# A chunked delta-rule kernel: the last step of the triangular inverse replaced by one residual correction

## The chip, the cores and the metric

The kernel runs on one core of one Trainium2 chip. A core has TensorE (PE, the matrix unit), VectorE (DVE), ScalarE (ACT), GpSimd (POOL) and SyncE (SP), each with its own instruction queue worked off in order, and 16 DMA engines. The metric is the device time of one execution in microseconds. Before the change it is 259.1 us (median of the runs; the lowest is 258.44 us).

## The reference: what is computed

For each of 4 × 8 heads with 768 time steps and 48 dimensions a state matrix is updated by the delta rule, and the outputs of all heads go through a feed-forward block of 384 → 2048 → 384 with a tanh-approximated GELU.

```python
k_n = k / (np.linalg.norm(k, axis=-1, keepdims=True) + 1e-06)
for t in range(S):
    y[:, :, t] = np.einsum('bhd,bhde->bhe', q[:, :, t], state)
    v_old = np.einsum('bhde,bhd->bhe', state, kt)
    state = state + bt[:, :, :, None] * np.einsum('bhd,bhe->bhde', kt, vt - v_old)
...
h = x @ w_in
g = 0.5 * h * (1.0 + np.tanh(c * (h + 0.044715 * h * h * h)))
return (g @ w_out).astype(np.float32)
```

`kt` is the normalised key of step t, `vt` the value, `bt` the scalar beta. Inputs and output are float32.

## The kernel before, in words

**Tiling.** Time is cut into 12 chunks of 64 steps (C = 64). A chunk holds 32 heads; 16 of them form a *unit*, two heads side by side on the two halves of the 128 partitions, so that there are 24 units, u = 2c and 2c + 1 for chunk c. Names in the code end in the unit (`A3.13`) or the chunk (`U.6`).

**Preparation of a unit (`load`, `norms`, `prep`).** q, k and v are loaded by DMA, the norms of k are computed, k is scaled, and everything is transposed, by PE (`T`, `kT`) or by a DMA transpose (`turn`). PE then makes the Gram matrices of the chunk: `G2` (keys with keys, its lower triangle kept by a DVE mask copy into `ln`, line 528) and `G` (keys with keys and with queries, upper triangle, mask copy into `wp`; in the first units separately, with `GQ` and `wpq`, or the ACT copy `wqa` and the POOL product `wqb`).

**The inverse.** Inside a chunk the delta rule is a triangular system (I + L) U = R. Its inverse is found by Newton's iteration in 5 steps, for every unit. The iterate is kept as a block-diagonal matrix `bd` (128 x 128 for each of 8 head pairs). `X10` and `X11` write the start (line 558, POOL, or line 560, DVE). Each step i is: `A{i}`, eight PE products of `bd` with a Gram matrix (line 569); `rt{i}`, a DVE instruction that forms 2I minus that (line 581); `B{i}`, eight products of `bd` with it (line 569); and copies out of PSUM back into `bd`: `bde` (two half copies, ACT or DVE, line 326), `bdf` (line 332), or `xi` (one copy) and then two `bdc` on POOL or DVE (line 611). Steps 4 and 5 work only on the columns that aren't exact yet: step 4 on 48 of 64, step 5 on 32. A form `J`, `C`, `rj` replaces `A`, `rt` in some places: PE puts 2I into PSUM first (line 587), and ACT or DVE copies.

**The chunk chain (`chain`).** From the state S of the chunk before: `K` (line 641) multiplies the state with the keys, `R` (DVE, line 654) forms the right-hand side `rb`, `U` (16 PE products of `bd` with `rb`, line 664) solves the system, `Un` copies it into `ub`, `S` (line 676) and `Sn` (DVE, line 683) form the next state, `Q` and `O` (lines 641 and 689) the output, `On` copies it, and it is transposed by PE (`X`, line 701, copy `xT`) or by DMA (`turnx`, line 706).

**The feed-forward block (`mlp`).** For each chunk 16 `up` products (line 718, three matmuls each), 4 `gelu` on ACT (line 722), 8 `down` (line 729, four matmuls each), copies `Z` and the DMAs out. The weights W1 and W2 are loaded by POOL's DMA queue (`w1`, `w2`, lines 435 and 437).

**The order.** The class `Flow` collects all operations with what they read and write. The string `ORDER` at the top (lines 17 to 105) lists all of them in one sequence; a suffix names the engine that is chosen (`:a` ACT, `:d` DVE, `:g` POOL, `:s` SP) or the PSUM bank (`@5`). Each engine's queue is that sequence cut down to its own operations, and `Flow.emit` adds the semaphore waits. There is no reordering at run time: an operation that waits holds up all behind it on its engine. PSUM has 8 banks; an operation that takes a bank waits until the last reader of the bank's earlier content is done. The `fill` products at the start only keep PE busy.

## Time and profile before

| | before |
|---|---|
| median of the runs | 259.1 us |
| profiled execution | 259.73 us |
| its span, first to last instruction | 258.0 us |
| granted TensorE clock, mean | 0.992 |
| busy: PE / DVE / ACT / POOL | 241.1 / 206.2 / 191.1 / 140.8 us |
| instructions | 12268 |

The profile shows one execution. The busy time of an engine is the union of its instructions; a PE matmul is drawn with its whole passage through the array, so that neighbours overlap, and the cost of a group on PE is read from the distance between starts. Idle time is put down to the instruction whose semaphore ended it ("<-"), and "issue" is a wait for which the profile shows no releaser. Line numbers are those of the kernel before. "PEld" is the loading of weights into the array, "SPq" and "ACTq" the queues that issue DMAs.

### The profile page before, as it was taken

What the parts mean: (1) busy time and instruction counts of PE and PEld (TensorE: products, weight loads), DVE (VectorE), ACT (ScalarE), POOL (GpSimd) and SP (SyncE); (2) the same over time, 40 slices, a digit from 0 to 9 for tenths busy, and PEclk for the clock granted to TensorE, in tenths of its full rate; (3) what the DMA queues carried; (4) which work ended last, traced back from release to release, by engine and by line L of the source; (5) the groups of instructions that cost most, each with busy time, mean ns of one, the idle gap of its engine ahead of it and who ended that gap; (6) DMA issues with size and microseconds to landing.
All of it is one profiled execution on the core that took longest, in us unless ns stands there. A gap on an engine that the chain in (4) does not pass through costs nothing.

```text
span 258.0 us, 12268 instructions
## 1 busy us (share of the span) xinstructions
PE 241.1 (93%) x5490; PEld 189.0 (73%) x5497; DVE 206.2 (80%) x354; ACT 191.1 (74%) x305; POOL 140.8 (55%) x205
## 2 busy tenths in 40 slices
PE   7878689979999999999999999999999999999994
PEld 2455568758877987887877887778868878878672
DVE  7889899979978989999889868889888889875100
ACT  4777789699987886996887887777946957655352
POOL 6679883889636797674595678455441322400000
PEclk9999979999999999999999999999999999999999
DMA  4999999994795997969939792239377123002122
GB/s 81 192 189 194 217 202 198 198 169 79 142 138 107 188 141 137 187 131 157 200 72 140 165 177 58 51 64 149 85 104 150 33 51 107 3 5 64 33 60 62
DMA packets 116788, 31.46 MB, mean 122 GB/s; under 512 B 110848, under 2 KB 115968, under 8 KB 116736
## 3 DMA queue, kind: packets, MB, share of 16 engines
q1 hardware_dynamic: 81136, 19.03, 47.6%
q10 hardware_dynamic: 32720, 8.51, 17.8%
q0 software_dynamic: 2880, 3.15, 7.2%
q8 instruction: 43, 0.70, 1.1%
q14 instruction: 9, 0.07, 0.1%
HBM read 20.64 MB, written 4.72 MB: 98 GB/s over the span
## 4 chain that ended last, share of the span: by engine, by line
PE 78%; DMA 6%; POOL 4%; ACT 4%; SPq 2%; DVE 2%; issue 2%; ACTq 1%; POOLq 0%
PE ps L729 24%; PE ps L718 23%; PE ps L569 20%; DMA kraw<-in_k_dram 3%; PE ps L524 3%; PE ps L641 3%; DMA qraw<-in_q_dram 2%; SPq L426 2%; PE ps L664 2%; PE ps L689 1%; PE ps L676 1%; ACT bd L326 1%; DVE rt L581 1%; POOL bd L558 1%; ACTq L426 1%
## 5 line engine op out<-in xcount | busy, mean ns | idle before, releaser
L326 ACT ACTIVATE bd<-ps 64x512 bf16<-64x512 f32 x122 | 70.6, 589 | 27.9 <-PE ps L569 26.0
L718 PE MATMUL ps<-xT,W 128*128 128x256 bf16 x576 | 77.5, 273 | 0.4 <-issue 0.2
L729 PE MATMUL ps<-W,gT 128*128 128x384 bf16 x384 | 74.1, 326 | 1.0 <-ACT wp L326 1.0
L722 ACT ACTIVATE gT<-ps 128x1024 bf16<-128x1024 f32 x48 | 48.0, 1019 | 14.9 <-PE ps L718 14.2
L581 DVE TENSOR_TENSOR rt<-ps,two 128x512 bf16<-128x512 f32 x70 | 47.5, 685 | 10.5 <-PE ps L569 9.4
L718 PEld LDWEIGHTS ps<-xT,W 128*128 128x128 bf16 x576 | 50.1, 98 | 6.9 <-issue 0.4
L729 PEld LDWEIGHTS ps<-W,gT 128*128 128x128 bf16 x384 | 32.8, 98 | 17.7 <-ACT wp L326 1.2
L558 POOL TENSOR_SCALAR_AFFINE_SELECT bd<-ln 64x512 bf16<-64x512 bf16 x40 | 26.6, 669 | 21.5 <-DVE ln L528 18.8
L611 POOL COPY bd<-xi 64x256 f32<-64x256 f32 x36 | 14.8, 415 | 34.7 <-ACT xi L326 26.9
L452 POOL TENSOR_TENSOR nrm<-nrm,half 128x16 f32<-128x16 f32 x9 | 26.3, 2920 | 6.5 <-DVE nrm L450 6.4
L569 PE MATMUL ps<-rt,bd 128*128 128x64 bf16 x576 | 28.1, 194 | 1.7 <-DVE rt L581 1.0
L569 PE MATMUL ps<-wp,bd 128*128 128x64 bf16 (+1 forms) x576 | 27.0, 188 | 1.9 <-ACT bd L332 0.6
L569 PEld LDWEIGHTS ps<-rt,bd 128*128 128x128 bf16 x576 | 23.3, 98 | 6.3 <-DVE rt L581 2.3
L528 DVE CAST_PREDICATED wp<-mup,ps 128x1024 bf16<-128x1024 uint16 (+1 forms) x25 | 27.6, 1107 | 0.5 <-PE ps L524 0.4
L569 PEld LDWEIGHTS ps<-wp,bd 128*128 128x128 bf16 x576 | 23.0, 97 | 5.0 <-ACT bd L326 0.7
L326 DVE CAST bd<-ps 64x512 bf16<-64x512 f32 x35 | 23.9, 685 | 2.6 <-PE ps L569 2.1
L581 DVE TENSOR_TENSOR rl<-ps,two 128x384 bf16<-128x384 f32 (+1 forms) x48 | 23.0, 486 | 3.6 <-PE ps L569 2.9
L479 POOL TENSOR_TENSOR tok<-kraw,nrm 128x384 bf16<-128x384 f32 x21 | 17.6, 840 | 8.9 <-PE ps L676 8.4
L332 ACT ACTIVATE bd<-ps,up 128x512 bf16<-128x512 f32 x29 | 19.6, 675 | 0.9 <-issue 0.4
L569 PE MATMUL ps<-ln,bd 128*128 128x64 bf16 (+1 forms) x384 | 18.7, 190 | 0.9 <-ACT bd L326 0.6
L528 DVE CAST_PREDICATED ln<-mlo,ps 128x512 bf16<-128x512 uint16 x24 | 16.4, 682 | 3.6 <-PE ps L524 3.3
L569 PE MATMUL ps<-rl,bd 128*128 128x64 bf16 x384 | 19.0, 194 | 0.2
(104 smaller groups left out, 344.1 us busy)
## 6 DMA issues: line engine op xcount, KB each, us to landing
qraw<-in_q_dram SPq DMA_DIRECT2D x16, 192.0 KB, 5.1
kraw<-in_k_dram SPq DMA_DIRECT2D x27, 96.0 KB, 4.0
vraw<-in_v_dram SPq DMA_DIRECT2D x26, 96.0 KB, 4.6
out_dram<-ob ACTq DMA_DIRECT2D x13, 192.0 KB, 3.2
vraw<-in_v_dram ACTq DMA_DIRECT2D x22, 96.0 KB, 4.2
out_dram<-ob SPq DMA_DIRECT2D x9, 192.0 KB, 3.6
kraw<-in_k_dram ACTq DMA_DIRECT2D x17, 96.0 KB, 4.3
qraw<-in_q_dram ACTq DMA_DIRECT2D x8, 192.0 KB, 5.9
```

What stands on the lines that cost most here:

```text
L326: return e.activation(out, in_, ACT.Copy) if e is nc.scalar else e.tensor_copy(out, in_)
L332: return e.activation(out, in_, ACT.Copy, scale=up1[:, 0:1]) if e is nc.scalar else e.tensor_scalar(out, in_, up1[:, 0:1], None, op0=ALU.mult)
L452: if e is nc.scalar else e.tensor_tensor(nr[:, 1, hx], nr[:, 0, hx], half[:, hx], ALU.pow), reads=[nrn, "half"] + ["one", "roots"] * (c < ...
L479: A(("dve", "pool"), op("kb"), lambda e, P: e.tensor_tensor(kb, kr, nr[:, 5, hx].unsqueeze(2).to_broadcast(full), ALU.mult), reads=[f"kraw ...
L528: return e.copy_predicated(out.rearrange("p (x g) t -> p x g t", x=2), mask[:, 0:wd].bitcast(U16).unsqueeze(1).unsqueeze(1).to_broadcast([ ...
L558: A(("pool", "dve"), op(f"X1{a}"), lambda e, P, src=ln[m][hf(a), :, :], dst=bd[b_][hf(a), :, hf(a)], a=a: e.affine_select(out=dst, in_=src ...
L569: ins = e.matmul(P(name)[:, C * h + cs.start:C * h + cs.stop], bd[b_][:, h, :], rhs[:, h, cs], **kw)
L581: A(("dve",), op(f"rt{i}"), lambda e, P, i=i, cs=cs, cn=cn, r_=r_: e.tensor_tensor(r_[:, :, cs], P(ps(f"A{i}")).rearrange("p (h t) -> p h ...
L611: A(("pool", "dve"), op(f"bdc{i}{a}"), lambda e, P, src=xi[i_][hf(a), :, :], dst=bd[b_][hf(a), :, hf(a)]: e.tensor_copy(dst.bitcast(F32), ...
L718: ins = e.matmul(P(ph)[:, 256 * f:256 * f + 256].rearrange("p (x t) -> p x t", x=2), W1[:, j, 128 * (i + f):128 * (i + f) + 128], x_[:, :, ...
L722: A(("act",), f"gelu{i // 4}.{c}", lambda e, P, i=i, ph=ph: e.activation(g_[:, i:i + 4, :], P(ph).rearrange("p (f t) -> p f t", f=4), ACT. ...
L729: ins = e.matmul(P(po)[:, 0:DM], g_[:, f, 128 * b:128 * b + 128], W2[:, f, :], start=(f == 0), stop=(f == FC - 1))
```

## The change

`RES` names the chunks 1 to 11. For their units the iteration makes 4 steps instead of 5. The start of the iteration comes from the upper mask copy (`wp`) instead of the lower one (`ln`), so that the sides alternate the other way round and step 4 works on the upper 48 columns. In the chain `U` now gives a first solution, which `Ua` (ACT or DVE) copies to `ub`. `M` (function `left`, 32 PE products of 64 x 64 weights) multiplies it with the masked Gram matrix in `wp`, `rd` (DVE) adds that to the right-hand side `rb`, so that `rb` becomes the residual, and `V` (the 16 products of `U` again) adds its correction into the PSUM banks of `U`, which stay taken until `Un` has copied them. Chunk 0 keeps its five steps.

`ORDER` is replaced as a whole: 1661 operations instead of 1727, in another sequence, with other choices of engine and bank. Among the choices: 5 `J` forms instead of 2, 7 `X` instead of 5 (so 5 `turnx` instead of 7), `wpq` on DVE for all of the first four units instead of `wqa` and `wqb` for three of them, 31 `fill` instead of 37, and many loads issued by SP that ACT issued before. The diff shows a few lines of the order and then the code.

```diff
--- before
+++ after
...
-up1.7 bdc50.17:d bdc51.17:g A2.19@5 up2.7 U.8@0 gelu2.7 bdc21.18:d Un.8:a A3.18@4 rt2.19 up4.7@6 up3.7 B2.19@5 rt3.18 S.8@0 B3.18@4 gelu0.7 up5.7 bde21.19:d
-On.8:a ln.21 qb.22:a G2.20@2 rt3.19 G.21@0 down02.7 ln.20 wp.21 B3.19@4 wp.20 down10.7@2 down11.7 X10.21:g A4.18@1 down12.7 bdf30.19:a rt4.18 X11.21:g A1.21@6
...
+rt3.14 k11.00:a gelu0.5 up8.5@4 rt2.15 up9.5 Ua.6:a M.6@6 v9.10:s up10.5 ln.16 k11.11:s out00.3:s B2.15@0 B3.14@1 up11.5 rd.6 xi3.14:d V.6 sq.10:g bdc30.14:g
...
+xi2.18:d up11.7 gelu2.7 bdc20.18:d up1.7 out00.5:s bdc21.18:d up2.7 up3.7 A2.19@0 pow.11 qb.22:g A3.18@1 U.8@6 up4.7@2 gelu0.7 rt2.19 B2.19@0 up5.7 rt3.18
+Ua.8:a vs.9:g B3.18@1 M.8@4 xi2.19:d bdc20.19:d xi3.18:a up6.7 rd.8 up7.7 Q.8@0 eps.11:g gelu1.7 qb.21:g V.8 Un.8:a bdc21.19:g bdc30.18:d A3.19@5 down10.7@4
...
+bdc40.23:d U.11@2 up1.10 Ua.11:a up2.10 up3.10 Z1.9:d Z0.9:a M.11@4 out11.9:s up4.10@6 up5.10 up6.10 rd.11 up7.10 gelu0.10 up8.10@0 V.11 up9.10 gelu1.10
...
@@ -270,6 +265,7 @@
     SPLIT = 4
     APART = 2
     ROOTS = 3
+    RES = range(1, NC)
     NR, NP, NB, NN, NI, NX, NG = 3, 6, 6, 4, 3, 3, 3
 
     F = Flow()
@@ -306,8 +302,8 @@
         tmpl = sb("tmpl", [128, 2 * C])
         bd = sb("bd", [128, H, 128], BF16, NB)
         rt = sb("rt", [128, H, C], BF16, NN)
-        rls = [sb(f"rl{i}_", [128, NN * H, C]) for i in range(2)]
-        rl = [[t[:, H * i:H * i + H, :] for i in range(NN)] for t in rls]
+        rls = [sb(f"rl{i}_", [128, (2 if i else NN + 2) * H, C]) for i in range(2)]
+        rl = [[t[:, H * i:H * i + H, :] for i in range(t.shape[1] // H)] for t in rls]
         xi = sb("xi", [128, H, C], BF16, NI)
         rs = sb("rs", [128, 2, 2, 4, D], BF16, 2)
         us = sb("us", [128, 2, 2, 4, D], BF16, 2)
@@ -374,11 +370,12 @@
                       e is not nc.gpsimd else e.tensor_copy(t[s][:, :, :].bitcast(F32), tmpl[:, 0:w].bitcast(F32).unsqueeze(1).to_broadcast([128, H, w // 2])),
                       reads=["tmpl", "tmplz"], writes=[f"{y}{s}" for y in n])
             for i in range(0 if s else 2):
-                lo, kc_ = 16 + 16 * i, slice(0, 32) if i else slice(C - 16, C)
-                A(EV, f"ladj{lo}", lambda e, P, i=i, lo=lo, kc_=kc_: e.activation(
-                    rls[i][:, :, kc_], tmpl[:, kc_].unsqueeze(1).to_broadcast([128, NN * H, lo]), ACT.Copy, scale=-1.0) if e is nc.scalar else
-                  e.tensor_scalar(rls[i][:, :, kc_], tmpl[:, kc_].unsqueeze(1).to_broadcast([128, NN * H, lo]), -1.0, None, op0=ALU.mult),
-                  reads=["tmpl"], writes=[f"rl{lo}{y}" for y in range(NN)])
+                lo = 16 + 16 * i
+                for y0, y1, kc_ in ((0, 2, slice(0, 32)),) if i else ((NN, NN + 2, slice(C - 16, C)), (0, NN, slice(0, 16))):
+                    A(EV, f"ladj{lo}{y0}", lambda e, P, i=i, lo=lo, kc_=kc_, y0=y0, y1=y1: e.activation(
+                        rls[i][:, H * y0:H * y1, kc_], tmpl[:, kc_].unsqueeze(1).to_broadcast([128, (y1 - y0) * H, lo]), ACT.Copy, scale=-1.0) if e is nc.scalar else
+                      e.tensor_scalar(rls[i][:, H * y0:H * y1, kc_], tmpl[:, kc_].unsqueeze(1).to_broadcast([128, (y1 - y0) * H, lo]), -1.0, None, op0=ALU.mult),
+                      reads=["tmpl"], writes=[f"rl{lo}{y}" for y in range(y0, y1)])
             if s < NB:
                 A(("dve", "pool"), f"bdz{s}", lambda e, P: e.memset(bd[s][:, :, :].bitcast(F32), 0.0), writes=[f"bd0{s}", f"bd1{s}"])
 
@@ -548,19 +545,19 @@
 
             bds = [f"bd{a}{b_}" for a in range(2)]
             xis = f"xi{i_}"
-            for i in range(1, 6):
+            for i in range(1, 5 if c in RES else 6):
                 if tiled:
                     if i == 1:
                         A(("dve", "pool"), op("X1"), lambda e, P: e.tensor_tensor(
                             xi[i_][:, :, :], ln[m][:, :, :], twob[:, :].unsqueeze(1).to_broadcast([128, H, C]), ALU.add), reads=[w("ln"), "twob"], writes=[xis])
                 elif i == 1:
                     for a in range(2):
-                        A(("pool", "dve"), op(f"X1{a}"), lambda e, P, src=ln[m][hf(a), :, :], dst=bd[b_][hf(a), :, hf(a)], a=a: e.affine_select(
+                        A(("pool", "dve"), op(f"X1{a}"), lambda e, P, src=(wp[s][hf(a), :, 0:C] if c in RES else ln[m][hf(a), :, :]), dst=bd[b_][hf(a), :, hf(a)], a=a: e.affine_select(
                             out=dst, in_=src, compare_op=ALU.not_equal, fill=1.0, base=0, pattern=[[0, H], [-1, C]],
                             channel_multiplier=1) if e is nc.gpsimd else e.tensor_tensor(
                             dst, src, twob[hf(a), :].unsqueeze(1).to_broadcast([64, H, C]), ALU.add),
-                          reads=[w("ln"), "twob"], writes=[bds[a]], upper=a == 1)
-                con, conn = (wp[s][:, :, 0:C], n("wpm")) if i % 2 else (ln[m], w("ln"))
+                          reads=[n("wpm") if c in RES else w("ln"), "twob"], writes=[bds[a]], upper=a == 1)
+                con, conn = (wp[s][:, :, 0:C], n("wpm")) if (i + (c in RES)) % 2 else (ln[m], w("ln"))
 
                 def product(e, P, name, rhs, cs, more=False):
                     kw = dict(start=False, stop=True, skip_group_check=True) if more else {}
@@ -572,10 +569,10 @@
                             ins = e.matmul(P(name)[hf(a), C * h + cs.start:C * h + cs.stop], xi[i_][hf(a), h, :], rhs[hf(a), h, cs], **kw)
                     return ins
                 pe, xs = (dict(mode="t", mm=2 * H), [xis]) if tiled else (dict(mode="m", mm=H), bds)
-                lo = {4: 16, 5: 32}.get(i, 0)
-                cs = {4: slice(0, C - 16), 5: slice(32, C)}.get(i, slice(0, C))
+                lo, m_ = {4: 16, 5: 32}.get(i, 0), m if c in RES else x + NN * (i == 4)
+                cs = {4: slice(16, C) if c in RES else slice(0, C - 16), 5: slice(32, C)}.get(i, slice(0, C))
                 cn = cs.stop - cs.start
-                r_, rn = (rt[m], w("rt")) if not lo else (rl[lo // 32][m], w(f"rl{lo}"))
+                r_, rn = (rt[m], w("rt")) if not lo else (rl[lo // 32][m_], w(f"rl{lo}") if c in RES else f"rl{lo}{m_}")
                 A(PE, op(f"A{i}"), lambda e, P, i=i, con=con, cs=cs, f=product: f(e, P, ps(f"A{i}"), con, cs), reads=xs + [conn], alloc=(ps(f"A{i}"), 1),
                   alt=(op(f"r{i}"), 0), **pe)
                 A(("dve",), op(f"rt{i}"), lambda e, P, i=i, cs=cs, cn=cn, r_=r_: e.tensor_tensor(
@@ -656,17 +653,34 @@
                     vr[:, :, :].rearrange("p (g y) d -> p y g d", y=2), ALU.add), reads=vrn, frees=[ps("K")], writes=[rbn + "a", rbn + "b"])
                 A(PE, op("Q"), lambda e, P: ks(e, P, 2, "O", 1), reads=n("kTq") + [son], alloc=(ps("O"), 2), mode="t", mm=32)
 
-            def umat(e, P):
+            def umat(e, P, more=False):
                 for x, g in each:
                     for p in range(2):
                         o = 512 * x + 4 * D * p + D * g
+                        kw = dict(start=not more and p == 0 and g == 0, stop=more, skip_group_check=True) if c in RES else {}
                         if not tiled:
-                            ins = e.matmul(P(ps("U"))[:, o:o + D], bd[us_[x] % NB][:, 4 * p + g, :], rb[:, p, x, g, :])
+                            ins = e.matmul(P(ps("U"))[:, o:o + D], bd[us_[x] % NB][:, 4 * p + g, :], rb[:, p, x, g, :], **kw)
                             continue
                         for a in range(2):
-                            ins = e.matmul(P(ps("U"))[hf(a), o:o + D], xi[us_[x] % NI][hf(a), 4 * p + g, :], rb[hf(a), p, x, g, :])
+                            ins = e.matmul(P(ps("U"))[hf(a), o:o + D], xi[us_[x] % NI][hf(a), 4 * p + g, :], rb[hf(a), p, x, g, :], **kw)
                 return ins
             A(PE, op("U"), umat, reads=inv + [rbn + "a", rbn + "b"], alloc=(ps("U"), 2), mode="t" if tiled else "m", mm=32 if tiled else 16)
+            if c in RES:
+                def left(e, P):
+                    for x, g in each:
+                        for p in range(2):
+                            for a in range(2):
+                                o = 512 * x + 4 * D * p + D * g
+                                ins = e.matmul(P(ps("M"))[hf(a), o:o + D], wp[ss[x]][hf(a), 4 * p + g, 0:C], ub[hf(a), x, p, g, :])
+                    return ins
+                A(EV, op("Ua"), lambda e, P: copy(e, ub[:, :, :, :, :].rearrange("p x y g d -> p x (y g d)"), banks(P(ps("U")))),
+                  reads=[ps("U")], writes=[ubn])
+                A(PE, op("M"), left, reads=n("wpm") + [ubn], alloc=(ps("M"), 2), mode="t", mm=32)
+                A(("dve",), op("rd"), lambda e, P: e.tensor_tensor(
+                    rb[:, :, :, :, :].rearrange("p y x g d -> p x y (g d)"), banks(P(ps("M"))).rearrange("p x (y r) -> p x y r", y=2),
+                    rb[:, :, :, :, :].rearrange("p y x g d -> p x y (g d)"), ALU.add), frees=[ps("M")], writes=[rbn + "a", rbn + "b"])
+                A(PE, op("V"), lambda e, P: umat(e, P, True), reads=inv + [rbn + "a", rbn + "b"], accum=[ps("U")],
+                  mode="t" if tiled else "m", mm=32 if tiled else 16)
             A(EV, op("Un"), lambda e, P: copy(e, ub[:, :, :, :, :].rearrange("p x y g d -> p x (y g d)"), banks(P(ps("U")))),
               frees=[ps("U")], writes=[ubn])
```

167 lines of the change are left out of this document (80 added, 87 removed).

## The prediction

> **What bounds the kernel now.** I read the page first, for the shares and the slices:
>
> ```profile
> PE 241.1 (93%) x5490; PEld 189.0 (73%) x5497; DVE 206.2 (80%) x354; ACT 191.1 (74%) x305; POOL 140.8 (55%) x205
> PE   7878689979999999999999999999999999999994
> PE 78%; DMA 6%; POOL 4%; ACT 4%; SPq 2%; DVE 2%; issue 2%; ACTq 1%; POOLq 0%
> ```
>
> TensorE is full in 32 of 40 slices and is 78% of the chain that ended last. The rest lies in the first slices. So next I asked for the busy time by stretch (columns: window, length, then busy us and count of PE, PEld, DVE, ACT, POOL, then clock, DMA share, GB/s):
>
> ```profile
> 0.00:20.00 20.00, 15.10 (x222) 8.16 (x225) 16.61 (x49) 13.31 (x28) 13.57 (x36) 1.00 1.09 155
> 20.00:40.00 20.00, 15.35 (x375) 12.35 (x379) 17.74 (x31) 15.88 (x30) 16.58 (x24) 0.91 1.25 204
> 80.00:100.00 20.00, 19.93 (x491) 16.34 (x491) 18.85 (x31) 17.23 (x30) 16.27 (x22) 1.00 1.00 148
> 160.00:180.00 20.00, 20.00 (x513) 15.73 (x512) 18.04 (x30) 15.71 (x26) 11.20 (x17) 1.00 0.49 76
> ```
>
> From 60 us to the end PE has next to no gap; in the first 40 us it idles 4.90 + 4.65 us, while DVE is busy 34.35 of 40 us and the DMA engines are saturated (a share over 1 is rounding of overlapping packets). Third, the waits of PE, first over the steady part (55 to 258 us), then the rows of PE around the end of start-up:
>
> ```profile
> PE ps L689 <- issue: 0.9, 1, 0.9
> PE ps L524 <- issue: 0.5, 1, 0.5
> PE ps L676 <- issue: 0.3, 1, 0.3
> 39.10 1.26 PE L718 MATMUL ps<-xT,W 128*128 128x256 bf16 x10
> 52.03 0.38 PE L641 MATMUL ps<-st,kT 48*64 48x48 bf16 x24 [0.61 <-issue]
> 53.79 1.47 PE L729 MATMUL ps<-W,gT 128*128 128x384 bf16 x8 [1.05 <-ACT wp L326]
> ```
>
> After 55 us PE waits 1.7 us in all. So there are two stages: a start-up of 39.1 us, until the first `up` product of the feed-forward part, set by DMA, DVE, ACT and POOL together, and then about 215 us in which the time is the sum of what PE is given, plus 1.66 us of stall near 53 us. An edit outside PE is worth nothing in the second stage unless it stalls PE.
>
> **What PE pays for each piece.** PE is pipelined, so what a group costs is the distance from its start to the next group's start, not its own length. One stretch holds nearly every kind that the change touches:
>
> ```profile
> 225.04 0.56 PE L664 MATMUL ps<-rs,bd 128*128 128x48 bf16 x16
> 225.45 0.39 PE L569 MATMUL ps<-rt,bd 128*128 128x64 bf16 x8
> 225.68 1.47 PE L729 MATMUL ps<-W,gT 128*128 128x384 bf16 x8
> 227.07 0.44 PE L641 MATMUL ps<-st,kT 48*64 48x48 bf16 x32
> 227.35 0.42 PE L676 MATMUL ps<-us,tok 64*64 64x48 bf16 x32
> 227.60 0.46 PE L689 MATMUL ps<-us,wp 64*64 64x48 bf16 x32
> 227.99 0.82 PE L729 MATMUL ps<-W,gT 128*128 128x384 bf16 x4
> 228.88 0.36 PE L569 MATMUL ps<-wp,bd 128*128 128x32 bf16 x8
> 229.10 0.49 PE L701 MATMUL ps<-ident,xo 128*128 128x128 bf16 x6
> 229.43 0.81 PE L729 MATMUL ps<-W,gT 128*128 128x384 bf16 x4
> 15.38 0.39 PE L587 MATMUL ps<-twob,ident 128*128 128x512 bf16 x1
> ```
>
> A5 (L569, 128x32): 229.10 − 228.88 = 0.22 us. A B step (64 columns): 225.68 − 225.45 = 0.23. U (L664, 16 matmuls): 0.41, so 25 ns each. S (L676, 32 small ones, all four 64x64 tiles in turn, followed by another tiled group): 0.25. O (L689, the same size, but followed by a full-array group): 0.39. So leaving the tiled form costs about 0.1 us. A transposition X: 0.33.
>
> **Part 1, the fifth step goes for 22 of 24 units.** PE loses 22 × (0.22 + 0.23) = 9.9 us, all of it in the second stage (the two units of chunk 0 keep it).
>
> **Part 2, the correction, 11 times.** V is U again on other data: 0.41. M is 32 matmuls of O's size, but with weights and outputs on the same half of the partitions, so it uses two of the four tiles, 16 matmuls in each. No row shows that. The lower bound is S, 0.25; the upper bound is no overlap at all, 32 × 25 ns = 0.81. I take 16 × 25 ns = 0.41 (nearest to U's spacing, one row of matmuls per tile) and 0.10 for the extra change of form: 0.51. Sum: 11 × (0.41 + 0.51) = +10.1 us; with the bounds +8.4 to +14.5.
>
> The Trainium skill (TensorEngine Tiling, Performance Considerations, Instruction Overhead) states about 60 cycles for each matmul on TRN2 however small its free size. If that were paid by each instruction of M in turn it would be, as an estimate at that skill's 2.4 GHz, 0.8 us for M, and the time would be 4 us longer; the 25 ns of A5 and U agree with it inside one tile, and S, at 8 ns a matmul over four tiles, shows that other tiles don't pay it again.
>
> **Part 3, what the new order changes on PE.** Counted in the two orders: two more chunks transpose by PE (7 X instead of 5, so two `turnx` fewer), 2 × 0.33 = +0.7; the J form (one 512-column matmul, L587, about 0.39) is used 5 times instead of 2, of which two fall behind the start-up: +0.8. The six fills fewer are warm-up in idle time: nothing. PE's second stage thus changes by −9.9 + 10.1 + 1.5 = +1.7 us.
>
> **Part 4, the other engines.**
>
> ```profile
> L581 DVE TENSOR_TENSOR rl<-ps,two 128x256 bf16<-128x256 f32 x24 | 9.8, 416 | 1.9 <-PE ps L569 1.5
> L326 ACT ACTIVATE bd<-ps 64x512 bf16<-64x512 f32 x122 | 70.6, 589 | 27.9 <-PE ps L569 26.0
> L326 ACT ACTIVATE us<-ps 128x768 bf16<-128x768 f32 x9 | 7.3, 808 | 1.0 <-PE ps L664 0.7
> L654 DVE TENSOR_TENSOR rs<-ps,vraw 128x768 bf16<-128x768 f32 x11 | 10.4, 949 | 0.4 <-PE ps L641 0.4
> ```
>
> DVE loses 22 × 0.416 = 9.2 us (rt5) and gains 11 × 0.949 = 10.4 (rd, sized like R on L654). ACT loses up to 44 half copies of 0.589 = 26 us (some were on DVE or POOL) and gains about nine Ua of 0.808. In the fullest stretch (80 to 100 us) DVE has 1.15 of 20 us free, so +1.2 over the run stays hidden under PE; ACT's relief frees nothing, as nothing on PE waits for ACT there. Without that cover the DVE term would cost its 1.2. The starting matrix of the iteration now comes from the wide mask copy instead of the narrow one, a fraction of a us later per unit, with other units' products on PE meanwhile: nothing.
>
> **Part 5, new waits.** U → Ua → M → rd → V → Un is a serial chain, and M and V sit in PE's queue: when one waits, all `up` and `down` behind it wait. The trace shows the hand-over times:
>
> ```profile
> 225.64 0.81 ACT L326 ACTIVATE us<-ps 128x768 bf16<-128x768 f32 x1 [0.68 <-PE ps L664]
> 227.87 0.96 DVE L683 TENSOR_TENSOR st<-ps,st 128x768 bf16<-128x768 f32 x1 [1.02 <-PE ps L676]
> ```
>
> U's last product was issued by 225.45 and its copy ended at 226.45, so 1.0 us plus a release: 1.05 of other PE work must stand between U and M. S was issued by 227.60 and the add ended at 228.83: 1.25 between M and V. By the costs above, the new order puts 0.9 to 2.2 us between U and M (shortest in chunks 6 and 11), 0.9 to 1.8 between M and V (shortest in chunk 8: `up6.7 up7.7 Q.8`), 0.8 to 1.6 between V and the next user of Un. Chunk by chunk the missing tenths add to 1.0 us, if ACT and DVE are free on time: +1.0, and not below 0. U's two PSUM banks are held some 3 us longer, and M takes two more; the order names the banks, so a late release is a PE wait too, part of the same term.
>
> **Part 6, start-up.** Both orders have PE at the same point of the units 2 and 3 when the first `up` comes, so only its moment matters.
>
> ```profile
> 13.91 0.71 POOL L326 CAST tok<-qraw 128x384 bf16<-128x384 f32 x1 [1.75 <-DMA qraw<-in_q_dram]
> 17.32 1.71 POOL L437 DMA_DIRECT2D W<-in_moe_w_out_dram x1
> 26.16 13.82 SPq L426 DMA_DIRECT2D kraw<-in_k_dram  x2
> W<-in_moe_w_out_dram POOLq DMA_DIRECT2D x2, 768.0 KB, 11.5
> W<-in_moe_w_in_dram POOLq DMA_DIRECT2D x2, 768.0 KB, 10.3
> ```
>
> POOL waited 1.75 us for q of chunk 0, ahead of chunk 0's first block-diagonal matrix; in the new order ACT makes that cast, and this wait can go. Against it, two mask copies of the query products come to DVE (ACT and POOL shared them before), which is the fullest engine here. I take −1.0 us. The ends are a gain of all that DVE idled in the first 40 us, 5.65, and the loss of the DMA rival below, 3.7. The 1.05 us of stall at 53.79 came from a copy on ACT (wqa.2) that the new order moves behind this point to DVE: −1.0; what is late next there is the K product, whose 0.61 I leave.
>
> **The sum.** +1.7 + 1.0 − 1.0 − 1.0 = +0.7 on the span of 258.0: 258.7. The profiled execution took 259.73, 1.73 more than its span, so 260.4; the median of the runs, 259.1, is 0.6 below it. Forecast: 259.8.
>
> **The rivals.** *Start-up gains (0.18).* PE idles most of the first 39 us, and ACT loses 8 of its 20 DMA issues and many copies there, so units may run closer together. If all of DVE's 5.65 us of idle goes, that is 4.65 more than I took: 255.2; with M at its lower bound (−1.8) 253.4. For it: PE's 9.5 idle us. Against it: DVE has more to do in start-up, not less.
>
> *The chain in the chunk stalls PE (0.13).* M and V are issued in a fixed place. If ACT or DVE reaches Ua, rd or Un a quarter of a us late in each of the 33 hand-overs, PE loses 33 × 0.25 = 8.2 us instead of 1.0: 267.0. It decides where PE's cover is under about 1.3 us; over half of the 33 places are below 1.5. Against it: before, U's one hand-over per chunk had 1.1 to 2.6 us of cover and cost nothing.
>
> *Loads come late (0.10).* Counted in the orders, 37 DMAs are issued on SP before the first `up` product (24 before) and 12 on ACT (20 before). SP's issue already stuck for 13.82 us for two loads. While the weights stream through POOL's queue (four transfers of some 11 us, two at a time, 22 us), the inputs held two of three queues with work, 14.7 us; with one of two it is 11, so the loads are 3.7 us later: 264.5 with the gain of part 6 gone. The Trainium skill (DMA: Bandwidth & Descriptors, Queues, rings and completion order) says that each DMA engine goes round-robin over the queue rows with work, which is this mechanism; no row here splits the share.
>
> *M without overlap (in the forecast's upper part):* +3.3, 263.1.
>
> **How the numbers follow.** The forecast's case has 0.59, its own range 256.5 to 263.0. A measurement here can tell about 2%, 5.2 us: faster is below 253.9, slower above 264.3. Start-up gains reach below 253.9 in most of their cases only together with M's lower bound or the other stalls gone: 0.13, and 0.02 from the forecast: 0.15. Slower: the chain 0.11, loads 0.05, M without overlap with a few waits 0.02: 0.18. Same: 0.67. The range leaves out the far parts of the chain and of the start-up: 254.0 to 265.5.
>
> **What would show it.** L569 falls by 352 matmuls; the new `left` product takes 0.4 to 0.5 us to the next start; PE's waits after 55 us stay under 3 us; the first L718 comes between 37 and 40 us. A first L718 past 42 us, or M and V heading PE's waits with more than 4 us, would make it wrong; so would a start-up below 35 us.

## The result, and the profile after

The kernel after takes 271.46 us (median of 4 runs, 268.99 to 274.55) against 258.77 us for the kernel before on the same chip: 1.0465 times, 95% interval 1.0368 to 1.0562. It is slower; 259.8 us and no change had been forecast. The profiled execution took 271.0 us, its span 269.3 us; before, 259.73 and 258.0. Some executions fall into a state in which the chip runs slower (one of these four of each kernel, and the profiled ones of e3, e11 and e13), so all ratios, and the times of the table and of the text on the experiments, are medians of the other runs, and from those three profiles is read only what an engine stood at, or where.

First the page of after: busy time and count of each engine, the slices of PE and of its granted clock, and the engines' shares of the chain that ended last.

```profile
PE 245.4 (91%) x5675; PEld 190.4 (71%) x5682; DVE 201.1 (75%) x339; ACT 179.9 (67%) x281; POOL 134.8 (50%) x202
...
PE   6796328999999999999979999999999999999994
...
PEclk9989658999999999999999999999999999999999
...
PE 80%; DVE 8%; DMA 5%; issue 2%; ACT 1%; POOL 1%; SPq 1%; ACTq 1%; POOLq 0%
```

PE has the hole that the forecast did not have: slices 5 and 6 (26.9 to 40.4 us) are at 3 and 2 tenths, and the clock there is at 6 and 5. Busy time by stretch (window, length, busy us and count of PE, PEld, DVE, ACT, POOL, then clock, DMA share, GB/s) gives the same:

```profile
20.00:40.00 20.00, 8.71 (x206) 6.73 (x206) 10.33 (x19) 9.45 (x18) 7.84 (x14) 0.73 1.09 188
40.00:60.00 20.00, 18.95 (x443) 15.14 (x442) 18.32 (x27) 14.89 (x24) 17.96 (x26) 0.93 0.83 138
80.00:100.00 20.00, 19.74 (x540) 15.88 (x538) 17.61 (x29) 17.37 (x29) 13.44 (x21) 1.00 0.86 140
160.00:180.00 20.00, 20.00 (x401) 15.77 (x387) 17.16 (x29) 14.14 (x21) 11.90 (x14) 1.00 0.57 105
```

Between 20 and 40 us every engine fell: PE 15.35 to 8.71, DVE 17.74 to 10.33, ACT 15.88 to 9.45, POOL 16.58 to 7.84. All of them wait for something. From 80 us on the stretches look as before. The rows of PE, last of start-up and a stretch late in the run:

```profile
46.75 0.36 PE L566 MATMUL ps<-wp,bd 128*128 128x48 bf16 x8
47.07 1.16 PE L732 MATMUL ps<-xT,W 128*128 128x256 bf16 x9
233.49 0.69 PE L674 MATMUL ps<-us,wp 64*64 64x48 bf16 x32
234.10 0.82 PE L743 MATMUL ps<-W,gT 128*128 128x384 bf16 x4
235.88 0.56 PE L662 MATMUL ps<-rs,bd 128*128 128x48 bf16 x16
236.28 0.81 PE L743 MATMUL ps<-W,gT 128*128 128x384 bf16 x4
```

The first `up` product (L732 now) starts at 47.07 us; before, at 39.10. That is 8.0 us of the 11.3 that the span grew. From there to the end it is 222.2 us against 218.9: 3.3 us more. M (L674) takes 234.10 − 233.49 = 0.61 us to the next start, V (L662) 0.40.

Who is waited for between 25 and 48 us (engine, line, releaser: us in all, times, longest), and below it the longest wait of PE in the whole run:

```profile
POOL tok L322 <- DMA qraw<-in_q_dram: 11.4, 1, 11.4
PEld ps L566 <- POOL bd L608: 8.6, 1, 8.6
ACT xi L322 <- PE ps L566: 8.3, 1, 8.3
DVE nrm L457 <- POOL nrm L453: 8.2, 1, 8.2
...
PE ps L566 <- POOL bd L608: 8.1, 1, 8.1
```

The chain of waits through that time (start, length, what):

```profile
20.86 2.17 SPq L423
23.04 0.04 issue
23.08 13.30 DMA qraw<-in_q_dram
...
36.51 0.50 POOL tok L322
37.01 0.80 POOL rs L643
37.81 0.34 POOL bd L608
```

It reads: a load of q for the third chunk (q2.1, the 24th issue on SP's queue) is issued at 23.08 and lands at 36.38; in before it was issued at 16.41 and landed at 23.53. POOL, which takes its work in the written order, stands at the cast of it (qb.5) for 11.4 us. Behind that cast in its queue (in before the cast stood behind the first `up` products) are the first chunk's right-hand side (L643) and the block-diagonal copies of a unit of the second chunk (L608), whose product is next in PE's queue. The work of the first two chunks thus waits for an input of the third.

Two things can have made that load late: its place on SP, behind 23 other issues, and what the queues got of the DMA engines. The second shows in the queues' share of the 16 DMA engines from 13 to 30 us (packets, MB, share; q0 carries the weights, q1 the loads of SP, q10 those of ACT). Before:

```profile
q1 hardware_dynamic: 6658, 1.25, 54.6%
q0 software_dynamic: 1278, 1.27, 46.1%
q10 hardware_dynamic: 4331, 0.81, 33.6%
```

After:

```profile
q0 software_dynamic: 1111, 1.81, 62.9%
q1 hardware_dynamic: 6303, 1.18, 47.7%
q10 hardware_dynamic: 578, 0.11, 4.5%
```

The inputs held two queues with work and got 2.06 MB; now they hold one and get 1.29. SP's queue did not take what ACT's gave up: the weights did, 46.1% to 62.9%. The round-robin over queue rows with work that the Trainium skill describes (DMA: Bandwidth & Descriptors, Queues, rings and completion order) would do this, and these rows agree with it. The weights were also issued closer together (three at 16.1, 20.4 and 24.2 us; before at 17.3, 23.1 and 29.6). e2, e3 and e7 below take these causes apart.

Last, PE's waits after 55 us:

```profile
PE ps L638 <- issue: 1.3, 1, 1.3
PE ps L703 <- issue: 0.6, 1, 0.6
PE ps L690 <- issue: 0.6, 1, 0.6
...
PE ps L521 <- DVE rs L679: 0.2, 1, 0.2
```

3.3 us in all (1.7 before). None of it is a wait of M or V for ACT or DVE.

### The profile page after: what moved, and what is told of

It reads as the page before. It is cut to its first block, busy times and chain, and to the rows that moved or that the text cites. A ratio compares the mean times of both kernels' runs of the same rounds, so it can differ in the third digit from the quotient of the medians.

```text
span 269.3 us, 12588 instructions
## 1 busy us (share of the span) xinstructions
PE 245.4 (91%) x5675; PEld 190.4 (71%) x5682; DVE 201.1 (75%) x339; ACT 179.9 (67%) x281; POOL 134.8 (50%) x202
## 3 DMA queue, kind: packets, MB, share of 16 engines
q0 software_dynamic: 2880, 3.15, 7.4%
## 4 chain that ended last, share of the span: by engine, by line
PE 80%; DVE 8%; DMA 5%; issue 2%; ACT 1%; POOL 1%; SPq 1%; ACTq 1%; POOLq 0%
PE ps L732 24%; PE ps L743 23%; PE ps L566 16%; DMA qraw<-in_q_dram 5%; PE ps L521 4%; PE ps L662 3%; PE ps L638 3%; PE ps L674 3%; PE ps L703 1%; DVE rt L578 1%; PE ps L690 1%; PE ps L485 1%; SPq L423 1%; PE ps L715 1%; DVE wp L322 1%
## 5 line engine op out<-in xcount | busy, mean ns | idle before, releaser
L732 PE MATMUL ps<-xT,W 128*128 128x256 bf16 x576 | 76.7, 273 | 0.0
L322 ACT ACTIVATE bd<-ps 64x512 bf16<-64x512 f32 x92 | 53.3, 588 | 19.7 <-PE ps L566 18.1
L732 PEld LDWEIGHTS ps<-xT,W 128*128 128x128 bf16 x576 | 50.6, 98 | 7.1 <-DVE ln L525 0.2
L578 DVE TENSOR_TENSOR rt<-ps,two 128x512 bf16<-128x512 f32 x67 | 45.0, 685 | 12.2 <-PE ps L566 11.8
L555 POOL TENSOR_SCALAR_AFFINE_SELECT bd<-wp 64x512 bf16<-64x512 bf16 x34 | 22.7, 668 | 28.3 <-DVE wp L525 25.7
L608 POOL COPY bd<-xi 64x256 f32<-64x256 f32 x44 | 18.1, 415 | 35.4 <-DVE xi L322 18.7
L566 PE MATMUL ps<-wp,bd 128*128 128x64 bf16 (+2 forms) x400 | 19.1, 190 | 9.4 <-POOL bd L608 8.1
L566 PEld LDWEIGHTS ps<-rt,bd 128*128 128x128 bf16 x576 | 23.1, 98 | 5.8 <-DVE rt L578 1.7
L566 PEld LDWEIGHTS ps<-wp,bd 128*128 128x128 bf16 x400 | 16.5, 99 | 12.9 <-POOL bd L608 8.6
L322 ACT ACTIVATE us<-ps 128x768 bf16<-128x768 f32 x19 | 15.4, 809 | 9.3 <-PE ps L662 9.2
L322 ACT ACTIVATE xi<-ps 128x512 bf16<-128x512 f32 x18 | 10.6, 595 | 12.2 <-PE ps L566 11.9
L566 PEld LDWEIGHTS ps<-ln,bd 128*128 128x128 bf16 x384 | 15.2, 98 | 4.5 <-ACT bd L322 1.9
L525 DVE CAST_PREDICATED ln<-mlo,ps 128x512 bf16<-128x512 uint16 x24 | 16.2, 680 | 1.9 <-PE ps L521 1.7
L322 DVE CAST bd<-ps 64x512 bf16<-64x512 f32 x25 | 17.0, 687 | 0.8 <-PE ps L566 0.2
```

What stands on the lines that cost most here:

```text
L322: return e.activation(out, in_, ACT.Copy) if e is nc.scalar else e.tensor_copy(out, in_)
L525: return e.copy_predicated(out.rearrange("p (x g) t -> p x g t", x=2), mask[:, 0:wd].bitcast(U16).unsqueeze(1).unsqueeze(1).to_broadcast([ ...
L555: A(("pool", "dve"), op(f"X1{a}"), lambda e, P, src=(wp[s][hf(a), :, 0:C] if c in RES else ln[m][hf(a), :, :]), dst=bd[b_][hf(a), :, hf(a) ...
L566: ins = e.matmul(P(name)[:, C * h + cs.start:C * h + cs.stop], bd[b_][:, h, :], rhs[:, h, cs], **kw)
L578: A(("dve",), op(f"rt{i}"), lambda e, P, i=i, cs=cs, cn=cn, r_=r_: e.tensor_tensor(r_[:, :, cs], P(ps(f"A{i}")).rearrange("p (h t) -> p h ...
L608: A(("pool", "dve"), op(f"bdc{i}{a}"), lambda e, P, src=xi[i_][hf(a), :, :], dst=bd[b_][hf(a), :, hf(a)]: e.tensor_copy(dst.bitcast(F32), ...
```

## The experiments

"First up", "second up" and "last up" are the starts of the first `up` product of the first, second and last chunk. All times in us.

| kernel | first up | second up | last up | span | median | ratio to before, interval |
|---|---|---|---|---|---|---|
| before | 39.1 | 61.4 | 243.9 | 258.0 | 258.4 | |
| after | 47.1 | 69.0 | 255.1 | 269.3 | 271.0 | 1.0465 [1.0368, 1.0562] |
| e1, cast later | 40.6 | 67.0 | 253.0 | 267.2 | 270.0 | 1.0454 [1.0355, 1.0552] |
| e2, load on ACT | 40.7 | 66.6 | 255.2 | 270.2 | 274.0 | 1.0557 [1.0478, 1.0636] |
| e5, start of before | 38.2 | 66.0 | 251.5 | 265.7 | 268.3 | 1.0358 [1.0289, 1.0426] |
| e6, no correction | 38.8 | 65.5 | 241.9 | 256.0 | 258.7 | 0.9965 [0.9922, 1.0007] |
| e7, loads on ACT | 37.8 | 65.8 | 251.9 | 266.0 | 268.1 | 1.0361 [1.0273, 1.0449] |
| e8, no fifth step | 38.9 | 60.0 | 238.2 | 252.4 | 254.6 | 0.9839 [0.9771, 0.9906] |
| e9, third chunk on | 39.2 | 63.8 | 251.2 | 265.4 | 267.4 | 1.0334 [1.0272, 1.0397] |
| e13, cast behind | | | | | 271.5 | 1.0488 [1.0370, 1.0606] |

**e1: the cast out of the way.** On POOL's queue the cast of the late q moves behind the copies for which PE waited.

```diff
-xi1.2:a qb.5:g bdf31.1:d ... bdc51.0:g bdc50.0:g inv.2
+xi1.2:a bdf31.1:d ... bdc51.0:g bdc50.0:g qb.5:g inv.2
```

> The changed kernel with one word of its order moved: the cast qb.5 (POOL, waits for q of chunk 2) goes from ahead of R0b.0 to behind the copies bdc50.0, so that chunk 0's last inverse step is no longer behind it on POOL. Theory (POOL's wait for a late q load is the start-up loss): the 8.1 us wait of PE on a POOL copy goes, the first up product comes at 39 to 41 us instead of 47.1, and the time is 262 to 265 us. Rival (the loads are late for everybody, so the next load only takes over; or the loss lies in the correction): the first up product stays beyond 44 us and the time falls by less than 3 us, to 268 or more.

The first `up` came at 40.6 us, as the theory had it, so the place of the cast is the cause of 6.5 of the 8 us at the start. But the time hardly moved, and 262 to 265 us was a miss: the second `up` came 26.4 us behind the first (22.3 before, 21.9 in after). The waits of e1 from 30 to 60 us show the next load in the same place:

```profile
POOL tok L322 <- DMA kraw<-in_k_dram: 5.0, 1, 5.0
...
DVE nrm L447 <- POOL sq L446: 3.5, 1, 3.5
PE ps L566 <- DVE rl L578: 3.4, 2, 3.1
```

**e2: that one load on ACT's queue.**

```diff
-q2.1:s
+q2.1:a
```

> The changed kernel with one DMA issued elsewhere: q2.1 (half of q of chunk 2) goes from SP's queue, where 23 issues stand before it, to ACT's, at the same place of the order. Theory (the load is late because it sits behind the others in the one queue that shares the DMA engines with the weights): it is issued near 17 us instead of 23, lands by 28 us instead of 36.4, POOL's wait falls from 11.4 us to under 3, and the time is 262 to 266 us. Rival (the weights fill the DMA engines whatever the queue): it lands after 33 us and the time stays over 268.

POOL starts the cast without a wait, although the weights keep their share from 13 to 30 us and the inputs get 1.39 MB, hardly more than in after:

```profile
24.60 0.50 POOL L322 CAST tok<-qraw 128x384 bf16<-128x384 f32 x1
q0 software_dynamic: 1165, 1.85, 63.1%
```

So the place of q2.1 on SP made it late enough to stop POOL: on ACT it is issued at 14.88. The time was a miss as in e1: first `up` at 40.7, then POOL waits 5.1 us for a k load, second `up` 25.9 us later, 274.0 us in all.

**e3: a weight transfer later.** `w2.1` moves behind `bdc50.0` on POOL's queue.

> The changed kernel with the third weight transfer (w2.1, 768 KB) issued by POOL behind the copies bdc50.0 instead of at 24.2 us. Theory (three weight transfers within 8 us keep the DMA engines from the loads): q of chunk 2 lands 3 to 6 us earlier, at 30 to 33 us, and the time falls by as much, to 265 to 268. Rival (the place in SP's queue alone makes it late): it lands within 1.5 us of 36.4 and the time falls by less than 2 us.

POOL still stood 8.0 us at the q load, but 11.4 in after: the load landed at 32.97 us, inside the 30 to 33 that the theory named, and the first `up` came at 43.7. So the weights beside it seem to slow the load as well. This is a sign and no proof, as the profile is one of the three named above, and the runs scatter from 268.4 to 275.4 us, so that the time decides nothing.

**e4: the exchange in the order of before.** The new operations are put by hand into the order of before, PSUM banks given out anew.

> The change itself with the order of before instead of the new one: step 5 is taken out for the units from 2 on, the two mask copies of a unit change places, Ua, M, rd and V are put in with 1.1 us or more of other PE work between them in nearly every chunk, and banks are reassigned where that forces it; all loads, weights and choices of engine stay as before. Theory (the correction costs PE 2 to 3 us and some waits, and the rest of the loss is the new order's start-up): the first up product comes at 38.5 to 40 us as before, and the time is 260 to 264 us. Rival (the correction's chain is what costs): first up as before and 267 us or more.

319.3 us (1.2321). The first `up` came at 39.7 as expected, but then PE idled 43 us in small waits. My order was bad, so e4 doesn't decide between theory and rival; it shows only what an order is worth.

**e5: the start of before.** The first 385 operations stand in the order of before (through the first `down` product), the rest in that of after.

> The change with the start-up of before: its first 385 operations stand in the order of before (through down00.0, with its loads, queues and engines; only step 5 of units 2 and 3 is left out and the two mask copies of a unit change places), and all that remains follows in the order of the changed kernel. Theory (the new order's start-up is what costs 8 us, the correction 3 us): the first up product comes at 38.5 to 40 us and the time is 260 to 264 us. Rival (the second stage of the new order costs the most by itself): 266 us or more.

A miss for the theory, 268.3 where 260 to 264 was expected, and the rival's number (266 or more). The first `up` is back at 38.2; 5.5 us of the gain go before the second one, and the rest of the run takes 3.1 us more than before.

**e6: e5 without the correction.** `Ua`, `M`, `rd` and `V` are left out for every chunk, so U keeps the error of an inverse of four steps.

```diff
-            if c in RES:
-                def left(e, P): ...
-                A(EV, op("Ua"), ...
-                A(PE, op("M"), ...
-                A(("dve",), op("rd"), ...
-                A(PE, op("V"), ...
```

> The same with the correction left out (Ua, M, rd and V of chunks 1 to 11 are gone, so the solution U stays with the error of four steps). Theory (part 2 of the sum: M 0.5 to 0.6 us and V 0.41 on a full PE): 10 to 12 us below the run with the correction, 249 to 253 us. Rival (the correction's waits cost as much as its products): 15 us or more below it. Rival (PE doesn't set the time there): less than 5 us below it.

9.6 us below e5, 0.87 us for each of 11 corrections; M and V by their groups are worth 0.61 + 0.41 = 1.02. So the correction costs no more than its matmuls: the chain U, Ua, M, rd, V stalls PE by next to nothing. The difference is nearly the expected one; the time itself is not (249 to 253), since e5 below it had missed. Without any correction, and with the fifth step gone, e6 is only as fast as before.

**e7: loads back on ACT.** In after, 16 loads of the second to the sixth chunk that ACT issued before are ACT's again, each at its place in the order.

```diff
-k2.10:s k2.00:s q1.1:s v2.11:s v2.10:s k3.10:s v2.01:s q3.0:s k4.10:s ...
+k2.10:a k2.00:a q1.1:a v2.11:a v2.10:a k3.10:a v2.01:a q3.0:a k4.10:a ...
```

> The changed kernel with 16 of its loads (of k, q and v of the chunks 1 to 5) issued by ACT, as before, instead of SP; nothing else changes place. Theory (with one queue the loads get a smaller part of the DMA engines beside the weights, and the queue's issue blocks): q of chunk 2 lands by 29 us instead of 36.4, the first up product comes by 41 us, no load holds POOL for over 2 us after it, and the time is 261 to 266 us. Rival (three weight transfers in 8 us are what delays the loads, whatever the queue): POOL still waits over 5 us for loads in sum, and the time is 268 us or more.

q2.1, still on SP but with five issues fewer ahead of it, is issued at 15.46 and lands at 23.19. The first `up` came at 37.8, 9.3 us earlier; the time fell by about 3 us, and the two intervals overlap. The queues from 13 to 30 us:

```profile
q0 software_dynamic: 729, 1.46, 45.9%
q1 hardware_dynamic: 4964, 0.93, 42.3%
q10 hardware_dynamic: 4871, 0.91, 40.7%
```

1.84 MB of inputs, and the weights are back at 45.9%, though three of them are issued within 8 us as in after (at 17.0, 20.2 and 25.0). So the issue on one queue made the inputs late; e7 changes place and share at once. For the rest of the run the rival was right on both of its signs: POOL waits over 5 us for a load, and the time is 268.1. What holds e7 up from 25 to 60 us is a k load of the fourth chunk, with POOL standing at its cast:

```profile
POOL tok L322 <- DMA kraw<-in_k_dram: 6.3, 1, 6.3
DVE nrm L447 <- POOL sq L446: 4.3, 1, 4.3
...
PE ps L566 <- DVE rl L578: 3.6, 2, 3.3
```

**e13: that cast moved as well.** On e7:

```diff
-qb.4:g kc.6:g ... bdz5:g sq.3:g vs.1:g ... kb.5:g ... kb.4:g
+qb.4:g ... bdz5:g vs.1:g ... kb.5:g kb.4:g sq.3:g kc.6:g
```

> The kernel with the 16 loads back on ACT, and on GpSimd's queue the cast of k of the fourth chunk (kc.6) and its squares (sq.3) moved behind vs.1, kb.5 and kb.4, which wait for no late load; nothing else differs. There GpSimd stood 6.3 us, to 39.5 us, for that k load, and then worked to 55.6 us without a gap, with kb.4 and kb.5, which the third chunk's transpositions need, at 44.9 to 47.8 us. Theory (the loss between the two up groups is the next late load, taken up in GpSimd's fixed order): kb.4 and kb.5 are done by about 40 us, the PE's wait of 3.3 us ahead of an inverse's product falls below 1 us, the second up group comes 22 to 24.5 us behind the first, and the time is 263.5 to 266 us. Rival (the loss is spread over ACT, DVE and half-clock stretches, or the next transfer takes over once more): the second up group still 26 us or more behind the first, 267 us or more.

No faster than e7 (271.5 us; the intervals overlap), as the rival had it. POOL now stood at the v of the second chunk:

```profile
PE ps L566 <- DVE rl L578: 7.4, 2, 7.2
POOL vraw L648 <- DMA vraw<-in_v_dram: 6.7, 1, 6.7
```

After each mending POOL stood at another late load: k of the fourth chunk in e1, e2 and e7, v of the second in e13. So more than one transfer comes late for its place in the order. The bytes don't say that the inputs as a whole are behind: by 45 us the queues of SP and ACT had moved 4.92 MB in before, 4.92 in after and 5.11 in e7. Only the weights were behind by then (3.15, 2.42 and 2.80 MB). By 60 us the two queues are at 7.64, 6.29 and 6.62 MB; whether that is cause or effect of the waits is not shown.

**e8: before without its fifth step.** The operations of step 5 are left out for units 2 to 23 and nothing takes their place, so the inverse stays unfinished.

> The kernel before with the fifth step left out for the units from 2 on (its A, rt, B and copies are gone and nothing else moves, so their inverse is left unfinished). Theory (part 1 of the sum, 22 x 0.45 us on a full PE): 9 to 11 us below before, 247.5 to 250 us. Rival (the time hangs on copies or chains more than on PE's products): less than 5 us below, 254 us or more.

254.6 us, 4.6 below before beside it (259.2), where 9 to 11 was expected: the rival's side. I counted every PE matmul (fills aside) at the mean spacing of its kind. So counted, e8 has 10 us less work than before, and 4.6 us more time that is not work (32.8 against 28.2 us to the last matmul). Nearly half of what the step costs comes back, most of it as short waits between groups: 7 of more than 0.25 us from 65 to 250 us, where before has 1.

**e9: the correction from the third chunk on.**

```diff
-    RES = range(1, NC)
+    RES = range(2, NC)
```

with the first 465 operations, through the transposition ahead of the second chunk's `up`, in the order of before.

> The correction from the third chunk on instead of the second; the second chunk's units 2 and 3 take their fifth step as before, and the first 465 operations, through the transposition ahead of the second chunk's up products, stand in the order of before; what follows stands in the order of after. Nothing is left out of the computation. Theory (the loss lies in the order of the first 66 us, 8 us ahead of the first up group and 5.5 us behind it once the first is mended; the exchange itself costs 3 to 4 us of the second stage): the first up group at about 39 us, the second chunk's at 61 to 62 (22 us behind it, as before), 185 us from there to the last chunk's, span 260.5 to 262, 261 to 263 us in all. Rival (the exchange itself makes the second chunk late, or the late loads only move on to the third chunk): the stretch ahead of the second chunk's up group is 22 us, but what follows takes 188 us or more: 265 us or more. If the order of after is only worse by its start, and the exchange is free, 258 to 260 us.

267.4: the rival's number, but not its two stretches. The second `up` is 24.5 us behind the first, where theory and rival had 22, and from there to the last it is 187.5 us, between the theory's 185 and the rival's 188. Two stretches at the seam of the two orders:

```profile
60.00:64.00 4.00, 2.21 (x58) 1.57 (x55) 3.25 (x5) 3.64 (x9) 0.42 (x2) 1.00 0.62 86
64.00:68.00 4.00, 4.00 (x36) 3.17 (x34) 1.74 (x3) 1.45 (x2) 2.90 (x4) 0.57 0.81 176
```

PE idles 1.8 us in four, then runs at 0.57 of its clock for the next four. The seam is mine, so e9 doesn't price the exchange in a good order.

**e10, e11, e12: the phase of PE's instructions.** In the records of after, holes of 0.3 to 1.5 us lie inside groups of matmuls that wait for nothing shown. The rows around the longest, and the instruction queue from 136 to 140 us:

```profile
137.35 0.33 PE L638 MATMUL ps<-st,kT 48*64 48x48 bf16 x17
139.03 0.31 PE L638 MATMUL ps<-st,kT 48*64 48x48 bf16 x15 [1.34 <-issue]
...
q8 instruction: 1, 0.02, 1.5%
```

That one packet of 16 KB came at 136.35, 8.2 us after the one before it. To test it, the first filling matmul becomes 64 (e10 on after, e12 on before) or 32 (e11 on after) small ones, which shifts all later instructions:

```diff
-e.matmul(P(n), wz[:, 0:128], wz[:, :])
+[e.matmul(P(n)[:, 0:32], wz[:, 0:128], wz[:, 0:32]) for _ in range(64)][-1]
```

> After, with 64 matmuls of 32 columns in place of the first filling matmul, so that 63 more pairs of weight load and matmul (126 instructions) stand ahead of all else on PE's queue; nothing else differs. After has five holes of 0.4 to 1.5 us inside a group of matmuls that waits for nothing the profile shows (1.53 us in K of the sixth chunk at 137.5 us, 0.79 in S, 0.80 in O, 0.43 in a Gram group), and each begins 1 to 2 us after a 16 KB packet of the instruction queue. Theory (the packet that brings the next instructions is late there): 126 instructions are about half of such a packet, so that every packet's edge moves to other matmuls: the hole in K of the sixth chunk goes, others come in other groups, their sum lies between 1 and 5 us (after: 4.2), and the time moves by what the sum moves by, 268.5 to 272.5 us. Rival (the holes belong to their groups: operands or banks): the same five holes at the same groups with the same lengths to 0.3 us, 271 to 272 us.

> The same with 32 small matmuls: 62 instructions more on PE's queue than in after, a quarter of a packet. Theory: the holes lie 30 matmuls or so earlier than in after, in part in the group ahead, and their lengths change; sum 1 to 5 us, 268.5 to 272.5 us. Rival: the same holes as in after, 271 to 272 us.

> Before, with the same 64 small matmuls in place of its first filling matmul. Before has holes of this kind of 0.41, 0.80, 1.04, 0.46 and 0.72 us, 3.4 us in all. Theory: they move to other groups and sum to 1 to 5 us: 256.5 to 261 us, a ratio of 0.99 to 1.01. Rival: the same holes in the same groups, a ratio of 1.00. If either kernel's time moved by more than 2%, part of the difference between before and after would be chance in where the packets' edges fall.

The holes moved. (The group that the expectations call K of the sixth chunk is its Q; both have line 638, and this one stands behind V and ahead of O.) In e10 it ran whole, 0.28 us to the next start; another hole cut a Gram group in two:

```profile
161.74 0.24 PE L521 MATMUL ps<-kT 48*64 48x128 bf16 x1
163.21 0.41 PE L521 MATMUL ps<-kT 48*64 48x128 bf16 x15 [1.24 <-issue]
```

Holes over 0.25 us behind 30 us sum to 4.2 us in after, 7.2 in e10 (above my 1 to 5), 3.7 in e11, 3.7 in before and 1.5 in e12. e10 took 275.0 us, above the 268.5 to 272.5 expected (1.0613 [1.0546, 1.0680]; after's 1.0465 has an interval that just reaches into it), with a span 4.1 us longer than after's, 3.0 of it in holes. e11 took 270.4 us (1.0455 [1.0377, 1.0534]), no change. e12 took 261.1 us (1.0105 [1.0076, 1.0134]) although it has fewer holes. Its second `up` came 24.1 us behind the first instead of 22.3: the granted clock was at half from 54.3 to 57.7 us, with PE busy all that time, where before ran at full, and that is 1.7 of the 1.8 us. So the holes go with the instruction stream, and e12 shows that 63 instruction pairs in idle time move the kernel before by about 1%. There the holes are not the reason; the clock is part of it, but since the profiled execution of e12 is only 0.4 us longer than that of before, the rest stays open.

## Why the prediction was wrong, point by point

**What bounds the kernel.** Right: a start-up, then a sum of PE work. The start-up moved by +8.0 us and the second stage by +3.3.

**Part 6, start-up: the step that failed.** −1.0 was taken, with +3.7 as the worst end; it was +8.0. I followed one cast on POOL (of the first chunk's q) that left its queue, and not the one that came into it ahead of the first chunk's work, qb.5. What the prediction had at nothing was the wait of PE behind that cast, 8.1 us. e1 and e2 show it: with that one cast or that one load moved, the first `up` is at 40.6 and 40.7. (A slip beside it: the order of before has 25 issues on SP ahead of the first `up`, not 24.)

**The rival "loads come late", 0.10.** It came nearest to what happened: one queue with work instead of two. e7 undoes it and has the first `up` at 37.8. Its price was mis-sized. It was a share of bandwidth: 14.7 us of queue time against 11. In bytes that was near: 2.06 MB fell to 1.29, and 0.77 MB at the 198 GB/s of before are 3.9 us. But e2 removes the wait while the inputs get next to no more of the DMA engines, so the place in the queue counted for more than the share, and a late load costs what stands behind it. q2.1 was the last of a row of 24 on SP and stood at the head of POOL's queue, so PE lost 8.1 us in one wait. With +8.0 in the place of −1.0 the sum of 260.4 is 269.4, and with the 1.6 by which the second stage exceeded its sum (below) 271.0, the time of the profiled execution, as it must be: the two stages make up the whole span.

**What I did not foresee at all:** that undoing it would bring 3 us at most and not 8. In after, all engines stand while the DMA engines go on, and after then has only 21.9 us from the first to the second `up`, with 0.4 us of idle PE. With the first wait gone (e1, e2, e5, e7) it is 25.9 to 28.0: PE idles 3.3 to 4.8 us of it, and in e1, e5 and e7 the clock is at half for 3.41 us, which costs 1.7 more. So most of the loss moves to the second chunk instead of going. That mending one of its places is enough is refuted four times; which of them sets the time in the end stays open, and an order planned anew with the loads on two queues was not tried.

**Parts 1 and 2.** M without a row to go by: 0.51 taken, 0.35 to 0.91 as ends in the sum (the rival at 263.1 counts its upper end without the change of form, as 0.81). It was 0.62 in nine chunks and 0.53 in two, where a tiled group follows: 6.7 us instead of 5.6, +1.1, a term too small though inside its ends. Within M a matmul starts 16.2 ns after the last (two tiles at work), so a tile takes one each 32 ns where U takes one each 26; the change of form was 0.1 as taken. V was 0.41 as taken. The 60 cycles for each matmul in turn (the Trainium skill, TensorEngine Tiling, Performance Considerations), which would have made M 0.8 us, are not borne out across tiles. The removed step was counted rightly as work (about 10 us), but e8 shows that time follows work only as far as the order has other work ready: 4 to 5 us came of it there.

**Parts 3 and 4.** The two J forms behind the start-up cost 0.22 us each to the next start, not 0.39, so +0.4 and not +0.8. DVE is less busy than before (201.1 against 206.2 us), and PE waits 0.2 us for it after 55 us.

**Part 5 and the rival "the chain stalls PE", 0.13.** +1.0 was taken. PE's waits after 55 us rose by 1.6, but 3.0 of the 3.3 are holes inside groups, of the kind of e10. The hand-overs of the correction cost next to nothing, by e6 against e5: 9.6 us for 11.2 us of matmuls.

**The second stage in sum:** +1.3 of work (the +1.7 with the J forms as measured), +1.1 for M, +1.6 of waits, −1.0 for the stall at 53.79 that went, together +3.0; measured +3.3. Part of it, up to the 3 us by which the holes of e10 and after differ, is chance of where instructions fall.

**Rivals "start-up gains" and "M without overlap":** no; the start-up lost, and M overlaps.

What the prediction named as its refutation is what came: a first L718 past 42 us. Of its other signs the 352 matmuls came; M took 0.62 us instead of 0.4 to 0.5, and PE's waits after 55 us are 3.3 instead of under 3.

## What to carry to other kernels

When a new order moves a load, look up two places: how many issues stand ahead of it in its queue, and what stands behind the instruction that first reads it on that engine. One cast of an input that the first `up` products don't need held PE for 8 us. Where the DMA engines are full, spread early loads over the issuing queues, so that none stands behind twenty others, and don't price a start-up by one wait: here the next late load took its place each time. And work that is taken off a full engine is worth its time only if the order has other work ready there; in e8 it was half.

## What the runs showed of the hardware

PE's instruction stream can hold PE up. Inside groups of matmuls there are 34 holes of over 0.5 us for which no releaser shows (behind 38 us, in the twelve kernels other than e3, e11 and e13). Of them 33 begin within 2.1 us of the start of a 16 KB packet of the instruction queue, and behind each of the 34 PE goes on 1.2 to 1.7 us after the packet's end (137.32 and 139.03 in after, 161.72 and 163.21 in e10). That they hang on the packet is inferred from this timing and from e10, where they moved with the stream. The Trainium skill (Runtime: NRT & Kernel Launch, Instruction fetch mechanics) calls the cost of crossing such a block mostly hidden; here that holds for most of the 45 packets of a run, and the others cost up to 2.1 us.

The granted clock changes in steps of 3.41 us (the clock's records in the trace). After ran at half for 13.65 us on end, from 29 to 43 us, around its wait of 8.1 us; in e9 an idle of 1.8 us in four was followed by one step at half, in which PE was busy throughout, which costs 1.7 us more (half of the step). A wait of PE can thus cost more than its length. The Trainium skill (TensorE: Matmul & The Clock Gate, Part 1) has windows of this length and asks for one that is idle; in e9 a window that was half idle was enough.
